# An adaLN block with a spectral filter: one slice of the modulation weights loaded in two parts, the second behind the fourth turning transfer

## The chip, the cores and the metric

The kernel runs on one core of a Trainium2 chip. The metric is the device time of one execution in microseconds; the time given for a kernel is the median of several runs. All times below are microseconds (us) from the start of the profiled span unless they are called device times.

## What is computed

A block with two branches, each with a layer norm, a modulation computed from a small vector `c`, and a gate, on x of 2048 tokens by 640 features in bf16:

```python
mod = (silu(c) @ w_mod).reshape(1, 6, 1, 640)
sa, ca, ga, sb, cb, gb = (mod[:, i] for i in range(6))
h = layernorm(x) * (1 + ca) + sa
y = irfft2(rfft2(h) * (w_r + 1j * w_i))          # over tokens and features
x = x + ga * y
h = layernorm(x) * (1 + cb) + sb
out = x + gb * ((silu(h @ w_gate) * (h @ w_up)) @ w_down)
```

`w_mod` has 640 rows and six slices of 640 columns. The order of the slices is sa, ca, ga, sb, cb, gb.

## The kernel before, in words

**Stages.** The two-dimensional Fourier transform is done by matrix products with cosine and sine tables. First comes the forward transform (loop at L482): tokens through `Mtab`, features through `Rs`, result `A_sb` in SBUF, 81 feature frequencies by 1024 values. Then `A_sb` has to be turned, so that the token frequencies lie in the free dimension. TensorE turns groups of four frequencies (`t2_pe`, L559), and four DMA transposes turn the rest (`t2_dma`, L539, issued at L549 to L552; called the four turning transfers here). Then a loop over 21 groups of up to four frequencies (L762) does the filter: `mix` (L577, matmuls at L583) into PSUM, `prod` (L599, VectorE at L607) times the filter weights, `stage_b` (L609, matmuls at L615, ScalarE copy at L618), `stage_c` (L633, matmuls at L645), `evac` (L647). GpSimd makes sums of weights (`wsum`, L421) and of products (`presum`, L621) in that time. A side line for the special frequencies runs in the same loop: `sp_gather` (L661, GpSimd at L663) reads all four turned pieces, then come `sp_mm` (L668) at groups 9, 11 and 13 and `sp_ev` (L691); its last step sends two small DMAs at L706 and L707. Then the inverse transform runs over 16 token tiles (L1258), each with a VectorE step at L1278 that adds the residual. After the third tile the second layer norm begins for the first two tiles, and at L1296 `ln2_tr(0)` issues a DMA transpose (line L878; called the h2 transpose here) whose result, modulated at L886 and L892, feeds the first products of the feed-forward part (`gu13`, L1090; `gu_plain`, L1102). The rest (L1132, L1003) is the feed-forward part in Strassen-like products, bound by TensorE.

**The modulation slices.** The vector `sc_col` is silu(c). `wm_ca` and `wm_sa` hold the slices of ca and sa. The other four lie in one tile `wm_r` of 5 x 4 x 640 (k block, slice, column) in the region rM: slice 0 is ga, 1 is sb, 2 is cb, 3 is gb. Slice 0 is used by `ga_mod` (L715, matmuls at L712). Slices 1 and 2 are used in pieces of 128 columns: in `mix`, behind the first matmul of a group, `mod_col` (L594, five matmuls at L596) makes one column piece `c5`, as this line orders it:

```python
for c5 in {8: (0,), 10: (1,), 12: (2,), 14: (3,), 16: (4,), 18: (5, 6), 20: (7, 8, 9)}.get(g, ()):
    mod_col(psum[:, 3 + 2 * (g % 2), 448 + c5:449 + c5], wm_r[:, :, 1 + c5 // NC5], c5 % NC5)
```

So group 8 reads columns 0 to 127 of slice 1, group 10 reads 128 to 255, group 12 reads 256 to 383, and so on; group 18 is the first to read slice 2. Slice 3 is read at the end of the loop (L814). `mix(g + 2)` is called in round g. TensorE takes its instructions in this written order.

**Queues.** Nearly all loads are issued by the SP queue, in the order of the program, and SP waits in order, too: an issue that waits for an engine holds back all issues behind it. The order around the change is: K tables, slice sa, slice 0, the special K table (L299), slice 1 (L300), then the four turning transfers (L549 to L552, all recorded at L543), the token table of the inverse transform (`Htab`, L553), its feature table (L554), slices 2 and 3 (L555, L556), the two small DMAs of the side line (L706, L707), the weights of the down product (L822 to L826), a small table (L829, L830), the gate and up weights (L834), the h2 transpose (L878). GpSimd issues some accumulating loads (L912).

Of the kernel before, what the change touches and what calls it, by code (L numbers as in the profile page):

```python
# [17 lines left out]
S, D, FF = 2048, 640, 1728  # L18
# [148 lines left out]
def adaln_block_kernel(ctx, tc, A_x, A_w_r, A_w_i, B_x, B_w_gate, B_w_up, B_w_down, c, w_mod, out):  # L167
    nc = tc.nc
# [57 lines left out]
    wm_r = rM.cut(12800, [NC5, 4, D])  # L226
# [68 lines left out]
    wm_m = wm_v[:, :, 2 * D:6 * D].rearrange("p k (i d) -> p k i d", i=4)  # L295
# [1 line left out]
    nc.sync.dma_start(wm_sa[:], wm_v[:, :, 0:D])  # L297
    nc.sync.dma_start(wm_r[:, :, 0, :], wm_m[:, :, 0, :])
    nc.sync.dma_start(Kstab[:], Ks_dram)  # L299
    nc.sync.dma_start(wm_r[:, :, 1, :], wm_m[:, :, 1, :])  # L300

    nc.vector.memset(ones[:], 1.0)
    nc.vector.memset(one11[:], 1.0)
# [29 lines left out]
    if True:  # L333
        def bn(ti, n=1, mid=None):
            for i in range(ti, ti + n):
                for k in range(2):
                    nc.vector.bn_stats(bn6a[:, i % 2, k, :], x_sb[:, i, 320 * k:320 * k + 320])  # L337
                    if i == ti + 1 and k == 0 and mid is not None:
                        if mid in (4,6,8):
                            xhat(mid, nc.vector)  # L340
                            xhat(mid + 1, nc.vector)
                        else:
                            xpair(mid)
            for i in range(ti, ti + n):
                nc.vector.bn_aggr(mv[:, i, :], bn6a[:, i % 2])
# [15 lines left out]
        def xpair(lo):  # L361
            nc.gpsimd.tensor_scalar(nmean[:, lo:lo + 2], mv[:, lo:lo + 2, 0], -1.0, 0.0, ALU.mult, ALU.add)
            xhat(lo, nc.gpsimd)
            xhat(lo + 1, nc.vector)

        def xhat(ti, eng):
            o, xi, r = xhs[ti // 2 % 3][:, ti % 2], x_sb[:, ti, :], rstd[:, ti:ti + 1]
            if eng is nc.vector:
                eng.tensor_scalar(o, xi, mv[:, ti, 0:1], r, ALU.subtract, ALU.mult)  # L369
            else:  # L370
                eng.tensor_scalar(o, xi, nmean[:, ti:ti + 1], r, ALU.add, ALU.mult)
# [80 lines left out]
        idle_pe(6, 2)  # L452
        nc.scalar.activation(sc_f[:], cps, ACT.Silu)
        bn(0, 2)
        rstd_of(0, 2)
        nc.vector.tensor_copy(sc_col[:], sc_f[:])
        mps = psum[:, 3, 32:32 + 32 * NC5]
        act_stats(3)
        for r in range(4):
            nc.scalar.mul(Rs[:, 1, r, :], Rp[:, 4, :], mask4[:, r:r + 1])  # L460
        bn(2)
        rstd_of(2, 1)
        xhat(0, nc.vector)
# [5 lines left out]
        xhat(2, nc.vector)  # L469
        xhat(3, nc.vector)  # L470
        bn(4, 2)
        idle_pe(4, 2)
        mod_cols(mps, wm_ca, range(0, 3), 32)
# [62 lines left out]
    if True:  # L536
        B2of = {}

        def t2_dma(bi):  # L539
            l0 = (1, 16, 32, 64)[bi]  # L540
            n = 15 if bi == 0 else 16
            B2b = rL.cut(4096 * bi, [16, 128]) if bi < 3 else rM.cut(6144, [16, 128])
            nc.sync.dma_start_transpose(B2b[:, :n, :], A_sb[:, l0:l0 + n].rearrange("p l t k c r -> p l (t k c r)"))  # L543
            for i in range(n):
                B2of[l0 + i] = (B2b, i)
            spec.append((B2b, n, slice(l0, l0 + n)))
# [3 lines left out]
        t2_dma(1)  # L550
        t2_dma(2)
        t2_dma(3)  # L552
        nc.sync.dma_start(Htab.rearrange("p (t h) v k -> p t h (v k)", h=2)[:, :, 0, :], H_dram.rearrange("p t v k -> p t (v k)"))  # L553
        nc.sync.dma_start(RI[:], RI_dram)  # L554
        nc.sync.dma_start(wm_r[:, :, 2, :], wm_m[:, :, 2, :])  # L555
# [808 lines left out]
@with_exitstack  # L1364
def kernel(
    ctx: ExitStack,
    tc: tile.TileContext,
    A_x: bass.AP,
    A_w_r: bass.AP,
    A_w_i: bass.AP,  # L1370
    B_x: bass.AP,
    B_w_gate: bass.AP,
    B_w_up: bass.AP,
    B_w_down: bass.AP,
    c: bass.AP,
    w_mod: bass.AP,
    out: bass.AP,
):
    with tc.manual_schedule():
        adaln_block_kernel(tc, A_x, A_w_r, A_w_i, B_x, B_w_gate, B_w_up, B_w_down, c, w_mod, out)  # L1380
# [30 lines left out]
```

## Time and profile before

| | us |
|---|---|
| median of 3 runs, device time | 247.27 (246.79 to 247.45) |
| the profiled execution, device time | 247.35 |
| its span in the profile | 245.6 |

The time outside the span is 247.35 - 245.6 = 1.75 us. Sums are made against the profiled execution. TensorE (PE) is busy for 96% of the span, VectorE (DVE) for 84%, ScalarE (ACT) for 69%, GpSimd (POOL) for 32%. "PEld" is TensorE's load of stationary weights, "SPq" the SP queue issuing.

### The profile page before, as it was taken

Reading aid. Unit: us, or ns where it says so; the run is one execution under the profiler, and the core shown is the slowest. Engines: PE = TensorE matmul, PEld = TensorE weight load, DVE = VectorE, ACT = ScalarE, POOL = GpSimd, SP = SyncE. Lnnn points to the kernel's source line nnn. Section 1 sums busy time; section 2 is a strip of 40 time slices with the busy share of each in tenths; the row PEclk is TensorE's granted clock in tenths of the full one; section 3 lists DMA queues with packets and bytes.
Section 4 is the critical chain, followed back from the end, with each engine's and each line's share of the span. In section 5 each row is a group of like instructions: output and inputs, shape, how many; then the busy total and the mean of one; then the engine's idle time right before and its main releaser. Section 6 shows DMA issues by size and latency. Waiting matters only on the chain.

```text
span 245.6 us, 5940 instructions
## 1 busy us (share of the span) xinstructions
PE 236.9 (96%) x2221; PEld 186.0 (76%) x2221; DVE 205.5 (84%) x485; ACT 170.2 (69%) x338; POOL 78.8 (32%) x122
## 2 busy tenths in 40 slices
PE   8899999899999999999999999999999999999994
PEld 2777889799997887788887778887765665666773
DVE  4898988797699995989989968788998777789864
ACT  3898877899997887588864588765247787773220
POOL 3637997698615414002004400001422000004400
PEclk9999999999999999999999999999999999999999
DMA  7999989989999899600005110202411000000111
GB/s 207 373 342 305 349 183 157 261 240 355 327 317 256 166 245 189 138 1 3 0 3 107 56 56 0 56 1 41 91 31 56 0 0 1 3 1 0 56 53 53
DMA packets 44142, 31.19 MB, mean 127 GB/s; under 512 B 21873, under 2 KB 41810, under 8 KB 44114
## 3 DMA queue, kind: packets, MB, share of 16 engines
q1 hardware_dynamic: 42176, 26.15, 41.2%
q0 software_dynamic: 1376, 4.26, 7.6%
q10 hardware_dynamic: 562, 0.41, 0.5%
q8 instruction: 17, 0.28, 0.5%
q14 instruction: 11, 0.09, 0.1%
HBM read 23.49 MB, written 2.62 MB: 106 GB/s over the span
## 4 chain that ended last, share of the span: by engine, by line
PE 79%; DVE 7%; POOL 5%; DMA 4%; issue 3%; ACT 0%; SPq 0%; DVEq 0%; POOLq 0%
PE psum L1132 36%; PE psum L1003 19%; PE psum L1102 6%; PE psum L980 3%; DMA rW<-rL 3%; DVE bn6a L337 3%; PE psum L615 2%; PE psum L583 2%; PE psum L1090 2%; PE psum L404 1%; DMA rX<-in_A_x_dram 1%; DVE rE L369 1%; PE psum L645 1%; POOL rL L1285 1%; DVE rM L607 1%
## 5 line engine op out<-in xcount | busy, mean ns | idle before, releaser
L1132 PEld LDWEIGHTS <-rW 128*128 128x128 bf16 (+1 forms) x429 | 42.0, 98 | 12.6
L1132 PE MATMUL psum<-rW 128*128 128x256 bf16 (+1 forms) x247 | 42.2, 287 | 0.0
L1029 POOL TENSOR_TENSOR rM<-rM,rL 128x320 f32<-128x320 f32 x6 | 5.4, 906 | 96.6 <-ACT rL L1028 96.6
L1003 PEld LDWEIGHTS <-rE 128*128 128x128 f16 (+1 forms) x196 | 19.0, 97 | 7.8
L1003 PE MATMUL psum<-rE 128*128 128x320 f16 (+1 forms) x147 | 22.9, 299 | 0.0
L607 DVE TENSOR_TENSOR rM<-psum,rW 128x384 bf16<-128x384 f32 (+2 forms) x42 | 20.4, 544 | 2.8 <-PE psum L583 2.8
L1170 ACT COPY rX<-psum 128x384 f32<-128x384 f32 (+2 forms) x27 | 14.0, 520 | 7.5 <-PE psum L1132 7.4
L1132 PEld LDWEIGHTS <-rE 128*128 128x128 f16 x156 | 15.3, 98 | 4.7
L1163 ACT COPY rH<-psum 128x384 f32<-128x384 f32 (+2 forms) x27 | 14.0, 517 | 7.0 <-PE psum L1132 6.3
L1167 DVE TENSOR_TENSOR rH<-psum,rM 128x512 bf16<-128x512 f32 (+1 forms) x24 | 15.0, 624 | 4.1 <-PE psum L1132 2.2
L1186 ACT ACTIVATE rL<-psum 128x384 bf16<-128x384 f32 (+2 forms) x27 | 14.4, 533 | 5.4 <-PE psum L1132 3.4
L1171 DVE TENSOR_TENSOR rX<-psum,rX 128x384 f32<-128x384 f32 (+2 forms) x27 | 16.3, 604 | 1.6 <-ACT rX L1170 1.4
L1157 ACT COPY rM<-psum 128x384 f32<-128x384 f32 (+2 forms) x27 | 13.9, 516 | 3.7 <-PE psum L1132 3.7
L1278 DVE SCALAR_TENSOR_TENSOR rM<-psum,rX 128x640 f32<-128x640 f32 x16 | 13.1, 821 | 3.8 <-PE psum L737 2.5
L1132 PE MATMUL psum<-rW,rE 128*128 128x256 bf16 (+1 forms) x78 | 15.6, 290 | 0.0
L1132 PE MATMUL psum<-rE,rY 128*128 128x256 f16 (+1 forms) x78 | 15.6, 290 | 0.0
L1187 ACT ACTIVATE rL<-rX 128x384 bf16<-128x384 f32 (+2 forms) x27 | 15.1, 558 | 0.0
L337 DVE BATCH_NORM_STATS2 bn6a<-rX 128x6 f32<-128x320 bf16 x30 | 13.1, 480 | 2.2 <-DMA rX<-in_A_x_dram 2.2
L1102 PE MATMUL psum<-rW 128*128 128x256 bf16 x130 | 14.4, 273 | 0.0
L972 DVE TENSOR_TENSOR rA<-psum,rM 128x320 bf16<-128x320 f32 (+1 forms) x27 | 12.1, 472 | 2.4 <-PE psum L980 2.3
L1102 PEld LDWEIGHTS <-rW 128*128 128x128 bf16 x130 | 12.7, 98 | 1.4
L424 POOL TENSOR_TENSOR rW<-rW 128x256 bf16<-128x256 bf16 x20 | 13.4, 700 | 0.7 <-DVE rW L393 0.5
(235 smaller groups left out, 640.0 us busy)
## 6 DMA issues: line engine op xcount, KB each, us to landing
rM<-in_w_mod_dram SPq DMA_DIRECT2D x4, 800.0 KB, 8.3
out_dram<-rA SPq DMA_DIRECT2D x31, 80.0 KB, 1.6
rX<-in_A_x_dram SPq DMA_DIRECT2D x6, 320.0 KB, 5.6
rA<-in_B_w_down_dram SPq DMA_DIRECT2D x2, 960.0 KB, 5.4
rY<-in_B_w_gate_dram POOLq DMA_DIRECT2D x2, 832.0 KB, 7.7
rW<-in_B_w_gate_dram SPq DMA_DIRECT2D x1, 1440.0 KB, 10.5
rW<-in_A_w_i_dram SPq DMA_DIRECT2D x2, 642.0 KB, 10.8
rW<-in_A_w_r_dram SPq DMA_DIRECT2D x2, 642.0 KB, 10.2
```

Source lines behind the costliest of these rows:

```text
L337: nc.vector.bn_stats(bn6a[:, i % 2, k, :], x_sb[:, i, 320 * k:320 * k + 320])
L607: nc.vector.tensor_tensor(PPs[g][:, v0:v1, hl], xv[:, v0:v1, hl], in1, ALU.mult)
L1003: nc.tensor.matmul(o, lhsT=lhs[rows(k), k], rhs=rhs[rows(k), k], start=start and k == ks[0], stop=stop and k == ks[-1], skip_group_check=True)
L1102: nc.tensor.matmul(gu[u], lhsT=Wgu[:, u, c5, ff * 128:(ff + 1) * 128], rhs=h2T[:, :, c5, :], start=(c5 == 0), stop=(c5 == NC5 - 1))
L1132: nc.tensor.matmul(o[:, f], lhsT=w, rhs=b, start=(start and f == 0 and i == 0), stop=(stop and f == len(groups[g]) - 1 and i == len(ops) - ...
L1157: nc.scalar.copy(c0, X)
L1163: nc.scalar.copy(c2, X)
L1167: nc.vector.tensor_tensor(c11, Z, c0, ALU.add)
L1170: nc.scalar.copy(c3, X)
L1171: nc.vector.tensor_tensor(c22, Y, c3, ALU.add)
L1186: nc.scalar.activation(g21, X, ACT.Silu, scale=-1.0)
L1187: nc.scalar.activation(g22, c22, ACT.Silu, scale=-1.0)
```

## The change

Slice 1 of `wm_r` is loaded in two parts: columns 0 to 255 in the old place, ahead of the turning transfers, and columns 256 to 639 right behind the fourth turning transfer, ahead of `Htab`. The other line of the diff only sets spaces in a tuple.

```diff
@@ -297,7 +297,7 @@
     nc.sync.dma_start(wm_r[:, :, 0, :], wm_m[:, :, 0, :])
     nc.sync.dma_start(Kstab[:], Ks_dram)
-    nc.sync.dma_start(wm_r[:, :, 1, :], wm_m[:, :, 1, :])
+    nc.sync.dma_start(wm_r[:, :, 1, 0:256], wm_m[:, :, 1, 0:256])
@@ -336,7 +336,7 @@
-                        if mid in (4,6,8):
+                        if mid in (4, 6, 8):
@@ -550,6 +550,7 @@
         t2_dma(2)
         t2_dma(3)
+        nc.sync.dma_start(wm_r[:, :, 1, 256:D], wm_m[:, :, 1, 256:D])
         nc.sync.dma_start(Htab.rearrange("p (t h) v k -> p t h (v k)", h=2)[:, :, 0, :], H_dram.rearrange("p t v k -> p t (v k)"))
         nc.sync.dma_start(RI[:], RI_dram)
         nc.sync.dma_start(wm_r[:, :, 2, :], wm_m[:, :, 2, :])
```

## The prediction

> **What bounds the kernel now.** I read the page's busy times first, then the chain of waits, then SP's issues with their landing times, then the DMA rate by stretches.
>
> ```profile
> PE 236.9 (96%) x2221; PEld 186.0 (76%) x2221; DVE 205.5 (84%) x485; ACT 170.2 (69%) x338; POOL 78.8 (32%) x122
> PE 79%; DVE 7%; POOL 5%; DMA 4%; issue 3%; ACT 0%; SPq 0%; DVEq 0%; POOLq 0%
> ```
>
> TensorE bounds the kernel. In the chain (second line) DMA holds 4%; most of that is one piece, seen in the chain in order of time (start, length, what):
>
> ```profile
> 69.49 7.04 DMA rW<-rL
> ...
> 80.20 14.19 PE psum L1102 x130
> ```
>
> From 80.20 on TensorE has work to the end, so what moves that start moves the end. Last to arrive ahead of it was the h2 transpose, issued at 69.49 and landed at 69.49 + 7.04 = 76.53. The timeline says how long TensorE waited for what follows from it:
>
> ```profile
> 79.27 0.38 PE L1090 MATMUL psum<-rW,Wp 128*128 128x256 bf16 x2 [0.61 <-POOL rW L886]
> ```
>
> So TensorE came 0.61 us before the modulated h2. Two paths meet here: TensorE's own, with 0.61 us to spare, and the h2 transpose, with nothing to spare. The change must be priced on both.
>
> Now the place of the change: SP's issues (start, length), with one line of SP's waits behind them.
>
> ```profile
> 24.80 0.71 SPq L300 DMA_DIRECT2D rM<-in_w_mod_dram  x1
> 32.44 7.70 SPq L543 DMA_TRANSPOSE rL<-rA  x3
> 40.31 3.08 SPq L543 DMA_TRANSPOSE rM<-rA  x1
> 43.44 0.65 SPq L553 DMA_DIRECT2D rH<-tab_H  x1
> ...
> 44.83 0.42 SPq L555 DMA_DIRECT2D rM<-in_w_mod_dram  x1
> 45.31 0.52 SPq L556 DMA_DIRECT2D rM<-in_w_mod_dram  x1
> 51.77 0.54 SPq L706 DMA_DIRECT2D rE<-rE  x1
> ...
> 53.07 1.12 SPq L822 DMA_DIRECT2D rA<-in_B_w_down_dram  x2
> ```
> ```profile
> SPq L543 <- DVE rA L419: 6.9, 1, 6.9
> ```
>
> The first turning transfer isn't held back in SP by slice 1: SP had issued slice 1 by 25.5 and then waited 6.9 us for VectorE to finish `A_sb`. Is it held back in the DMA engines? I compare it with a transpose on an idle queue much later (windows: length, PE, PEld, DVE, ACT, POOL busy, clock, DMA share, GB/s):
>
> ```profile
> 32.44:33.64 1.20, 1.20 (x27) 1.07 (x24) 0.54 (x4) 1.14 (x3) 0.67 (x2) 1.00 0.05 13
> 129.55:130.72 1.17, 1.17 (x11) 0.73 (x9) 1.10 (x4) 0.57 (x2) 0.03 (x1) 1.00 0.00 0
> ```
> ```profile
> 129.55 3.10 SPq L878 DMA_TRANSPOSE rW<-rL  x1
> ```
>
> The transpose issued at 129.55 moves nothing for 1.17 us either, with nothing ahead of it. The first turning transfer waits about 1.2 us, in which the rest of slice 1 drains (13 GB/s). So slice 1 is out of the way before the transfers could begin, and taking 60% of it away frees at most some 0.1 us. That is the main point against a gain.
>
> Do the turning transfers matter? Yes, the fourth:
>
> ```profile
> 45.20 0.97 POOL L663 TENSOR_TENSOR rE<-rM,SA 128x16 bf16<-128x16 bf16 x6 [1.24 <-DMA rM<-rA]
> ```
>
> GpSimd waits 1.24 us for it, and TensorE for GpSimd. Were the transfers late because of slice 1, up to about 1 us could be won. By the windows above they aren't.
>
> **The change part by part.** *Removed from the front:* 384 of 640 columns, 800 x 0.6 = 480 KB, ahead of the transfers. Its readers had it long before. I cost this at 0 (bounds: 0.1 us gained by the windows above; nothing lost).
>
> *First part, 320 KB, read by groups 8 and 10.* Does group 8 now wait for the second part as well, being the same tile? Slice 0 answers (start, length):
>
> ```profile
> 36.26 0.84 PE L712 MATMUL psum<-rM,sc_rep 128*128 128x320 bf16 x5
> ```
>
> These products read slice 0 at 36.26, though the loads of slices 2 and 3 into the same tile stand ahead of them in the program and were issued only at 44.83 and 45.31. Waits go by the columns. Cost 0.
>
> *Second part, 480 KB, issued at 43.44 where `Htab` was.* When does it land, and when is it wanted? Landing times of `Htab`, its follower and slice 2 (KB, us from issue), then TensorE's weight loads:
>
> ```profile
> rH<-tab_H SPq DMA_DIRECT2D x1, 512.0 KB, 4.8
> ```
> ```profile
> rH<-tab_RI SPq DMA_DIRECT2D x1, 320.0 KB, 5.0
> ```
> ```profile
> rM<-in_w_mod_dram SPq DMA_DIRECT2D x1, 800.0 KB, 8.1
> ```
> ```profile
> 47.39 0.25 PEld L596 LDWEIGHTS <-rM 128*128 128x128 bf16 x5
> ...
> 48.55 0.21 PEld L645 LDWEIGHTS <-rY 128*128 128x128 bf16 x3 [0.22 <-issue]
> ...
> 53.64 0.38 PEld L596 LDWEIGHTS <-rM 128*128 128x128 bf16 x10
> ...
> 54.31 0.26 PEld L615 LDWEIGHTS <-rE 128*128 128x128 bf16 x4 [0.16 <-POOL rE L624]
> ```
>
> The L596 rows are in order: group 8, 10, 12 and so on; the one at 47.39 is group 12, the first to read column 256. `Htab` in this slot landed at 43.44 + 4.8 = 48.24. The second part has 32 KB less, at 353 GB/s (a row below) 0.09 us: 48.15. TensorE then waits 48.15 - 47.39 = 0.76 us. Bounds: 0, if it lands within 3.95 us; and 1.05 us, with the 5.0 us of the row behind `Htab`. I take 0.76, since the slot and the size are `Htab`'s.
>
> Queued behind that matmul on TensorE are the rest of group 12's `mix`, `stage_b` and `stage_c`. `stage_c` had its own gap of 0.22 us at 48.55, which vanishes into the new wait: net 0.76 - 0.22 = 0.54.
>
> The Trainium skill ("DMA: Bandwidth & Descriptors", the section on the anatomy of one DMA) fits one DMA as about 2.0 us plus bytes over 436 GB/s. For the second part that would be an estimate of 3.1 us, so 46.6, and no wait at all; for `Htab` it would be 3.2 us, and this trace shows 4.8. The measurement decides, and the page's result is a rival below.
>
> *The queue behind it.* `Htab`, RI and slices 2 and 3 come later by what 480 KB take. Rates (last column, GB/s):
>
> ```profile
> 45.00:46.00 1.00, 0.36 (x7) 0.19 (x4) 0.43 (x1) 0.75 (x2) 0.80 (x6) 1.00 0.34 47
> 46.00:52.00 6.00, 5.68 (x99) 5.51 (x100) 5.03 (x16) 4.97 (x10) 5.23 (x9) 1.00 1.07 353
> 53.00:54.00 1.00, 1.00 (x25) 1.00 (x23) 1.00 (x4) 1.00 (x3) 1.00 (x2) 1.00 0.24 29
> 54.00:55.00 1.00, 1.00 (x20) 0.84 (x17) 1.00 (x4) 0.76 (x3) 1.00 (x2) 1.00 0.67 56
> 55.00:72.00 17.00, 16.94 (x280) 15.82 (x277) 12.68 (x31) 15.37 (x30) 10.02 (x13) 1.00 1.09 348
> 72.00:76.00 4.00, 4.00 (x62) 3.73 (x61) 3.70 (x9) 3.79 (x9) 0.00 (x0) 1.00 1.35 120
> ```
>
> 480 KB are 0.49 MB; at 353 GB/s, 1.39 us. The extra issue on SP (0.42 to 0.71 us by its neighbours' rows) hides in that. `Htab` then lands at 48.24 + 1.39 = 49.6; its first reader is GpSimd, much later:
>
> ```profile
> 54.24 1.11 POOL L785 TENSOR_SCALAR rH<-rH,sgnc 128x1024 bf16<-128x1024 bf16 x1
> ```
>
> So 0 for `Htab`; RI is read after it, slice 3 only behind the last group. Slice 2 is tight: it landed at 44.83 + 8.1 = 52.93 and comes at 54.32; group 18 wants it at 53.64 + 0.54 = 54.18. Another 0.14 us. TensorE then is 0.68 us late, and the gap of 0.16 at 54.31 can take back some: I take 0.6. Bounds: 0, if what makes the second part land in time brings slice 2 forward, too; and 1.05, the upper end of the first wait with no gap that takes any back (slice 2 is in time then).
>
> The Trainium skill (same page, Bandwidth) wants loads batched to 1 MiB or more and gives 341 GB/s at 1 MB and 138 at 64 KB. By it the split loses rate; at an estimated 240 GB/s the 480 KB would take 2.05 us. Here the loads of 320 to 800 KB in 46 to 52 run at 353, so the trace disagrees.
>
> *Does the delay reach the h2 transpose?* From 55 to 72 the DMA engines run full (DMA share 1.09), and the transpose's data come only after that (120 GB/s from 72 on): a queue that starts later drains later. But at 53 to 55 it moves only about 85 KB in 2 us; at 353 GB/s that leaves (706 - 85) / 353 = 1.76 us free. SP issued nothing between 45.31 and 51.77, and the down weights only at 53.07; with 1.2 us to first data, as in the windows above, they couldn't flow before 54.3. I read the pause as a queue run dry, and 1.39 fits into 1.76. What then moves the 55 us start is SP: the DMA at 51.77 waits for VectorE's step below, and VectorE, busy for 5.03 of the 6 us from 46 to 52, takes that step behind its products of group 12:
>
> ```profile
> 51.34 0.29 DVE L705 CAST rE<-psum 128x40 bf16<-128x40 f32 x2
> ```
>
> TensorE's 0.54 passes through VectorE to SP nearly whole, so the down weights and all behind them come about 0.5 us later, and the h2 transpose lands 0.5 us later (bounds 0 and 1.39). TensorE's own 0.6 fits into the 0.61 us it had to spare. L1090 therefore starts 0.5 later, and so does the end.
>
> **Sum:** 247.35 + 0.76 - 0.22 (the gap), with the 0.14 of slice 2 lost in TensorE's spare time, is 247.35 + 0.5 = 247.85. The profiled execution stands 0.08 above the median of 247.27; for a median I say 247.8.
>
> **The rivals.** *The queue passes it on (slower).* Place: the pause at 53 to 55. If more than 1.76 - 1.39 = 0.37 us of it are start-up that recurs however full the queue is, the rest adds up; if all of it recurs, the h2 transpose comes 1.39 late: 247.27 + 1.39 = 248.7. For it: the other slow second, 45 to 46 at 47 GB/s, had loads waiting (issued 43.44 to 45.31) and wasn't dry. Against: the 1.2 us to first data explain most of the pause.
>
> *No trace left.* The second part lands within 3.95 us, as the skill's fit has it; the slow second at 45 to 46 would have to be `Htab`'s own. Then neither path moves: 247.3.
>
> *The transfers come earlier (faster).* If slice 1's tail holds the first turning transfer by up to 0.9 us in spite of the idle-queue row, the 1.24 us wait shrinks by as much, and TensorE is 0.9 - 0.6 = 0.3 early. The end gains only if the h2 transpose, too, is earlier, and at most 0.61 + 0.3 = 0.9: about 246.4.
>
> *It doesn't act by columns.* Group 8, whose turn comes in the round of L663 (45.20), waits for the second part until 48.15: 3 us or more, 250 and up. The L712 row speaks against it.
>
> **How the numbers follow.** About 0.3% (0.74 us) can be told from no change. Forecast (247.4 to 248.3): 0.52, of which 0.15 lies above 248.0. Queue passes it on: 0.22. No trace left: 0.15. Faster: 0.09. Not by columns: 0.02. Faster 0.09; same 0.37 + 0.15 = 0.52; slower 0.15 + 0.22 + 0.02 = 0.39. The range takes in the first three, from 247.0 to 249.0 (0.3 beyond the second case).
>
> **What would show it.** Right: L596 of group 12 with a wait on the second part near 0.8 us; the fourth transfer's wait at L663 still 1.2; the pause at 53 to 55 filled; L1090 at about 79.8 still waiting for L886. Wrong: a first turning transfer that moves data before 33.5; no wait at L596; or a pause as long as before, with the h2 transpose landing near 77.9.

## The result, and the profile after

| | before | changed |
|---|---|---|
| median, first comparison (6 runs each) | 246.83 (246.24 to 247.45) | 248.99 (248.74 to 249.96) |
| ratio, first comparison | | 1.0077 [1.0049, 1.0106] |
| median, second comparison (23 and 10 runs, below) | 246.78 (246.17 to 248.06) | 248.08 (246.90 to 250.26) |
| ratio, second comparison | | 1.0059 [1.0033, 1.0086] |
| profiled execution, device time | 247.35 | 249.0 |
| its span | 245.6 | 247.2 |

The change costs 1.3 to 2.2 us. The forecast was 247.8 and the range 247.0 to 249.0: the direction was right, the size too small. The first median stands 0.01 us below the upper end of the range, so that it lies inside is luck; the second, 248.08, lies well inside.

I read the profile after in the order of the prediction. First the page's busy times and the shares of the chain that ended last:

```profile
PE 237.8 (96%) x2221; PEld 186.2 (75%) x2221; DVE 205.7 (83%) x485; ACT 170.0 (69%) x338; POOL 78.7 (32%) x122
...
PE 80%; DMA 9%; DVE 4%; POOL 3%; issue 1%; ACT 1%; SPq 0%; ACTq 0%; DVEq 0%; POOLq 0%
```

No engine has more work to speak of, but DMA's share of the chain went from 4% to 9%. The changed kernel's chain around the change, in order of time (start, length, what), says what is new in it:

```profile
43.33 5.31 DMA rM<-in_w_mod_dram
...
48.68 0.28 PE psum L597 x5
```

The second part of slice 1 now lies on the chain: issued at 43.33, landed 5.31 us later at 48.64, and TensorE's group 12 (L596 is L597 after) goes on with it. The timeline of TensorE's weight loads gives the wait in brackets:

```profile
48.67 0.19 PEld L597 LDWEIGHTS <-rM 128*128 128x128 bf16 x5 [1.40 <-DMA rM<-in_w_mod_dram]
...
50.61 0.26 PEld L597 LDWEIGHTS <-rM 128*128 128x128 bf16 x5
...
54.60 0.38 PEld L597 LDWEIGHTS <-rM 128*128 128x128 bf16 x10
```

It is 1.40 us, where 0.76 was forecast. The next piece, group 14 at 50.61, comes 0.96 later than in before:

```profile
49.65 0.26 PEld L596 LDWEIGHTS <-rM 128*128 128x128 bf16 x5
```

Groups 8 and 10 show no such wait (waits go by the columns), and group 18, at 54.60, none on slice 2. How it goes on is seen in SP's issues, a line later in the code than before:

```profile
40.23 3.06 SPq L543 DMA_TRANSPOSE rM<-rA  x1
...
52.73 0.54 SPq L707 DMA_DIRECT2D rE<-rE  x1
54.12 1.12 SPq L823 DMA_DIRECT2D rA<-in_B_w_down_dram  x2
70.43 1.99 SPq L879 DMA_TRANSPOSE rW<-rL  x1
```

The fourth turning transfer (40.23) is issued as in before (40.31). The two small DMAs come at 52.73 instead of 51.77 (0.96 later), the down weights 1.05 later, the h2 transpose 0.94 later. The chain at the end of that stretch, and TensorE's timeline there:

```profile
69.87 0.53 DVE rL L865
...
70.43 7.92 DMA rW<-rL
...
78.54 2.40 POOL rW L887 x4
...
80.98 0.38 PE psum L1091 x2
```
```profile
79.68 0.27 PE L1091 MATMUL psum<-rW,Wp 128*128 128x256 bf16 x1 [0.27 <-POOL rW L887]
80.44 0.27 PE L1091 MATMUL psum<-rW,Wp 128*128 128x256 bf16 x1 [0.49 <-POOL rW L887]
80.98 0.38 PE L1091 MATMUL psum<-rW,Wp 128*128 128x256 bf16 x2 [0.27 <-POOL rW L887]
```

The chain comes to the h2 transpose from VectorE's step of the second layer norm (L865), not from an issue of SP: it is issued late because TensorE, and behind it the layer norm, are late. The transpose took 7.92 us instead of 7.04. So it lands 0.94 + 0.88 = 1.82 later, at 78.35 instead of 76.53, the matmuls behind it come 80.98 - 79.27 = 1.71 later, and the device time is 249.0 - 247.35 = 1.65 longer. TensorE, although late itself, still waits 0.27 + 0.49 + 0.27 = 1.03 us there: it isn't its own lateness that sets the end.

The DMA rate by stretches in the changed kernel (last column GB/s), for the pause and for the first turning transfer:

```profile
32.34:33.54 1.20, 1.20 (x27) 1.08 (x24) 0.55 (x3) 1.14 (x3) 0.67 (x2) 1.00 0.02 7
54.00:55.00 1.00, 1.00 (x24) 1.00 (x23) 1.00 (x4) 1.00 (x2) 1.00 (x2) 1.00 0.39 70
55.00:56.00 1.00, 1.00 (x20) 0.84 (x17) 1.00 (x3) 0.83 (x3) 1.00 (x2) 1.00 0.57 77
```

With 480 KB less ahead of it, the first turning transfer still moves nothing for its first 1.2 us (7 GB/s, before 13). GpSimd's wait for the fourth transfer is the same, too (1.24 before; timeline of GpSimd):

```profile
45.11 0.98 POOL L664 TENSOR_TENSOR rE<-rM,SA 128x16 bf16<-128x16 bf16 x6 [1.26 <-DMA rM<-rA]
```

The pause is still there: before it was 53 to 55 at 29 and 56 GB/s, now 54 to 56 at 70 and 77. That alone doesn't say that the 480 KB found no room in it, for SP issues the down weights 1.05 us later, which by itself would lengthen the pause. The bytes are counted under e2 below.

### The profile page after: what moved, and what is told of

Same layout as the page of the kernel before. It is cut to its first block, busy times and chain, and to the rows that moved or that the text cites. A ratio compares the mean times of both kernels' runs of the same rounds, so it can differ in the third digit from the quotient of the medians.

```text
span 247.2 us, 5943 instructions
## 1 busy us (share of the span) xinstructions
PE 237.8 (96%) x2221; PEld 186.2 (75%) x2221; DVE 205.7 (83%) x485; ACT 170.0 (69%) x338; POOL 78.7 (32%) x122
## 4 chain that ended last, share of the span: by engine, by line
PE 80%; DMA 9%; DVE 4%; POOL 3%; issue 1%; ACT 1%; SPq 0%; ACTq 0%; DVEq 0%; POOLq 0%
PE psum L1133 36%; PE psum L1004 19%; PE psum L1103 6%; DMA rX<-in_A_x_dram 4%; DMA rW<-rL 3%; PE psum L981 3%; PE psum L616 3%; PE psum L584 2%; DMA rM<-in_w_mod_dram 2%; DVE bn6a L337 2%; PE psum L1091 2%; PE psum L646 1%; PE psum L404 1%; POOL rL L1286 1%; POOL rW L887 1%
## 5 line engine op out<-in xcount | busy, mean ns | idle before, releaser
L619 ACT CAST rY<-psum 128x512 bf16<-128x512 f32 (+2 forms) x21 | 11.9, 576 | 3.5 <-PE psum L616 3.3
```

## The experiments

My theory after the result: two costs, both of which reach the end by the h2 transpose. *The wait*: group 12 holds TensorE, hence VectorE and SP, and the down weights are issued late. *The bytes*: 480 KB more stand in the queue ahead of the h2 transpose, and it takes longer from issue to landing. The rivals: the wait alone (the prediction's forecast), the bytes alone ("the queue passes it on"), and a cost of splitting as such.

| run | median, us (runs) | before beside it | ratio |
|---|---|---|---|
| e1_split_ahead | 247.11 (12) | 246.84 | 1.0013 [1.0002, 1.0025] |
| e2_read_later | 247.71 (6) | 246.84 | 1.0041 [1.0025, 1.0058] |
| e3_behind_htab | 249.42 (6) | 246.84 | 1.0108 [1.0074, 1.0142] |
| e4_up_behind_h2 | 246.88 (12) | 246.84 | 0.9998 [0.9985, 1.0011] |
| e5_htab_first | 247.59 (12) | 246.85 | 1.0029 [1.0018, 1.0040] |
| e6_split384 | 247.20 (12) | 246.85 | 1.0008 [0.9996, 1.0021] |
| e7_before_up_behind_h2 | 246.38 (12) | 246.85 | 0.9988 [0.9973, 1.0002] |
| e8_later_up_behind_h2 | 246.19 (12) | 246.85 | 0.9973 [0.9960, 0.9985] |
| e9_change_again | 248.08 (10) | 246.78 | 1.0059 [1.0033, 1.0086] |
| e10_wait_up_behind_h2 | 247.47 (7) | 246.78 | 1.0020 [1.0000, 1.0040] |
| e11_small_table_behind_h2 | 246.51 (12) | 246.78 | 0.9993 [0.9982, 1.0003] |

**Splitting alone.** Both parts stay ahead of the turning transfers.

```diff
     nc.sync.dma_start(wm_r[:, :, 1, 0:256], wm_m[:, :, 1, 0:256])
+    nc.sync.dma_start(wm_r[:, :, 1, 256:D], wm_m[:, :, 1, 256:D])
...
-        nc.sync.dma_start(wm_r[:, :, 1, 256:D], wm_m[:, :, 1, 256:D])
```

> Slice 1 in two parts, both ahead of the turning transfers. Theory 'the wait' (TensorE waits at group 12 for the second part, and the loop, SP and the h2 transpose follow it): no wait, so the time of before, 246.8 +-0.4. Theory 'the queue' (0.49 MB behind the fourth transfer push all later loads, whatever TensorE does): also 246.8 +-0.4, since nothing is moved behind the transfers. If the split itself costs (rows of 512 and 768 bytes, one DMA more): 247.5 or more.

Measured 247.11, 0.27 us above before by the medians (at most 0.6 by the interval) for one more DMA. The rest of the cost lies in the place of the second part.

**The bytes without the wait.** The change, but the column piece 2 is made in group 14 instead of group 12, when the second part has long landed.

```diff
-                    for c5 in {8: (0,), 10: (1,), 12: (2,), 14: (3,), 16: (4,), 18: (5, 6), 20: (7, 8, 9)}.get(g, ()):
+                    for c5 in {8: (0,), 10: (1,), 14: (2, 3), 16: (4,), 18: (5, 6), 20: (7, 8, 9)}.get(g, ()):
```

> The changed kernel, with the column piece 2 made in group 14 beside piece 3, not in group 12; the loads stay as changed. 'The wait': TensorE wants column 256 about 2.2 us later, by when it has landed; the loop is on time, so the small DMAs at L707 come at about 51.8 and the time is 247.0 +-0.4. 'The queue': the 0.49 MB are still ahead of everything, the h2 transpose lands 1.4 us or more later than before, 248.3 to 249.

Measured 247.71, 0.87 above before, with no wait at the modulation products. That is between the two numbers expected and fits neither. SP's down weights and the chain's transpose in this kernel:

```profile
53.49 1.12 SPq L823 DMA_DIRECT2D rA<-in_B_w_down_dram  x2
```
```profile
69.97 7.64 DMA rW<-rL
```

I measure how much longer the h2 transpose is held by the time from the down weights' issue to its landing, which leaves out how late SP was. Before: 76.53 - 53.07 = 23.46. Here: 69.97 + 7.64 - 53.49 = 24.12, which is 0.66 us more. "The wait alone" falls. The split alone (e1), with nothing pushed back, has 68.72 + 7.06 - 52.21 = 23.57:

```profile
52.21 1.12 SPq L823 DMA_DIRECT2D rA<-in_B_w_down_dram  x2
```
```profile
68.72 7.06 DMA rW<-rL
```

Do the 0.66 us arise because the pause doesn't take the bytes up? The windows answer, laid by the down weights' issue: from 45.00 to 1.5 us behind that issue, the next 6 us, and the next 5.5 us; in before, in this kernel and in the changed kernel.

```profile
45.00:54.57 9.57, 8.61 (x150) 8.03 (x148) 8.03 (x23) 8.27 (x14) 8.60 (x16) 1.00 0.88 264
54.57:60.57 6.00, 6.00 (x127) 5.87 (x125) 5.04 (x11) 5.22 (x10) 5.73 (x5) 1.00 0.98 340
60.57:66.07 5.50, 5.44 (x83) 5.00 (x81) 2.69 (x7) 5.09 (x12) 2.30 (x5) 1.00 1.15 294
```
```profile
45.00:54.99 9.99, 8.89 (x153) 8.44 (x153) 8.43 (x24) 8.57 (x14) 8.70 (x16) 1.00 1.02 302
54.99:60.99 6.00, 6.00 (x126) 5.87 (x124) 5.07 (x11) 5.36 (x10) 5.62 (x5) 1.00 1.01 339
60.99:66.49 5.50, 5.27 (x81) 4.88 (x77) 2.63 (x7) 4.92 (x11) 2.22 (x5) 1.00 1.18 281
```
```profile
45.00:55.62 10.62, 8.62 (x149) 7.91 (x147) 8.11 (x23) 8.18 (x14) 8.69 (x16) 1.00 0.92 282
55.62:61.62 6.00, 6.00 (x127) 5.87 (x125) 4.95 (x11) 5.28 (x9) 5.66 (x5) 1.00 0.99 341
61.62:67.12 5.50, 5.48 (x84) 5.00 (x82) 2.77 (x8) 5.11 (x12) 2.40 (x5) 1.00 1.13 246
```

The first rows moved 9.57 x 264 = 2526, 9.99 x 302 = 3017 and 10.62 x 282 = 2995 thousand bytes: 491 and 469 more than before, and 480 KB are 492. So nearly all pushed bytes have moved within 1.5 us of the down weights' issue, as in the prediction, and the 6 us behind that run at 340, 339 and 341 GB/s, alike. The queue falls behind only in the third stretch, at 294, 281 and 246. For the changed kernel that is 5.5 x (294 - 246) / 340 = 0.78 us, all that it is late by this measure (78.35 - 54.12 = 24.23, against 23.46: 0.77). For e2 it is 0.21 of the 0.66; the rest isn't placed. The same stretch in two kernels further down that push nothing back, e7 and, with the small table (L829, L830) behind the h2 transpose as well, e11:

```profile
60.15:65.65 5.50, 5.48 (x83) 5.00 (x81) 2.69 (x7) 5.12 (x12) 2.31 (x5) 1.00 1.16 252
```
```profile
59.91:65.41 5.50, 5.48 (x83) 5.00 (x81) 2.69 (x7) 5.11 (x12) 2.31 (x5) 1.00 1.09 336
```

e11 differs from e7 in the place of the small table alone, so the stretch is slow when that table's loads are in it. But e7, with no bytes pushed back, is nearly as slow there as the changed kernel. That the second part costs time without any wait of TensorE is shown by e2's median; by what way 480 KB that have long moved would slow that stretch is not.

**The wait without the bytes.** `Htab` (512 KB) takes the place of the second part ahead of the transfers, so that behind them stands nearly as much as before (32 KB less).

```diff
+    nc.sync.dma_start(Htab.rearrange("p (t h) v k -> p t h (v k)", h=2)[:, :, 0, :], H_dram.rearrange("p t v k -> p t (v k)"))
     nc.sync.dma_start(wm_r[:, :, 1, 0:256], wm_m[:, :, 1, 0:256])
...
         nc.sync.dma_start(wm_r[:, :, 1, 256:D], wm_m[:, :, 1, 256:D])
-        nc.sync.dma_start(Htab.rearrange("p (t h) v k -> p t h (v k)", h=2)[:, :, 0, :], H_dram.rearrange("p t v k -> p t (v k)"))
```

> The changed kernel, with the token table (512 KB) issued ahead of the turning transfers, in front of the first part of slice 1: ahead of the transfers stand 32 KB more than before the change, behind them 32 KB less, so the wait of TensorE is left alone without bytes pushed back. Theory 'both halves' (the wait costs about 1.1 us, the bytes in the queue about 0.9): TensorE waits 0.8 to 1.4 us at group 12 and the time is 1.1 above before, 247.9 +-0.4. 'The wait' alone as cause: 249.0. 'The queue' alone: 246.8.

Measured 247.59, 0.74 above before. Its weight load of group 12, its down weights and its h2 transpose:

```profile
48.08 0.19 PEld L597 LDWEIGHTS <-rM 128*128 128x128 bf16 x5 [0.73 <-DMA rM<-in_w_mod_dram]
```
```profile
53.49 1.12 SPq L823 DMA_DIRECT2D rA<-in_B_w_down_dram  x2
```
```profile
70.12 6.90 DMA rW<-rL
```

The wait is there, 0.73 us, and 70.12 + 6.90 - 53.49 = 23.53: the h2 transpose is held no longer than in before (23.46) and e1 (23.57). "The bytes alone" falls, too. The two costs together, 0.87 + 0.74 = 1.61 us, lie between the 1.30 and the 2.16 of the two comparisons of the change.

**Fewer bytes, no wait.** The cut at column 384: 320 KB go behind the transfers, and group 12 finds its columns in the first part.

```diff
-    nc.sync.dma_start(wm_r[:, :, 1, 0:256], wm_m[:, :, 1, 0:256])
+    nc.sync.dma_start(wm_r[:, :, 1, 0:384], wm_m[:, :, 1, 0:384])
...
-        nc.sync.dma_start(wm_r[:, :, 1, 256:D], wm_m[:, :, 1, 256:D])
+        nc.sync.dma_start(wm_r[:, :, 1, 384:D], wm_m[:, :, 1, 384:D])
```

> The changed kernel, cut at column 384, not 256: 480 KB ahead, 320 KB behind the fourth transfer, first read by group 14, 2.2 us later than group 12. No wait of TensorE, 0.33 MB pushed back. 'Both halves': two thirds of the queue's 0.9 us, 247.4 +-0.4. 'The wait' alone: 246.9. 'The queue' alone (2.1 us for 0.49 MB): 248.2.

Measured 247.20, 0.35 above before by the medians; the interval takes in no change, so the time alone doesn't part the 247.4 of both halves from the 246.9 of the wait. Its rows:

```profile
52.39 1.12 SPq L823 DMA_DIRECT2D rA<-in_B_w_down_dram  x2
```
```profile
68.80 7.69 DMA rW<-rL
```

68.80 + 7.69 - 52.39 = 24.10: the h2 transpose is held as long as with 480 KB. The size of the bytes' cost doesn't follow their number in single profiles; that they cost something is shown by e2 against before, how much per KB isn't.

**A longer wait.** The second part behind `Htab`.

```diff
-        nc.sync.dma_start(wm_r[:, :, 1, 256:D], wm_m[:, :, 1, 256:D])
         nc.sync.dma_start(Htab.rearrange("p (t h) v k -> p t h (v k)", h=2)[:, :, 0, :], H_dram.rearrange("p t v k -> p t (v k)"))
+        nc.sync.dma_start(wm_r[:, :, 1, 256:D], wm_m[:, :, 1, 256:D])
```

> The changed kernel, with the second part issued behind the token table, not ahead of it: the same bytes in the same stretch of the queue, but the second part lands some 1.4 us later (about 50). 'The wait': TensorE waits 2.7 us instead of 1.3 and the time is 1.2 to 1.5 us above the changed kernel, about 250.3. 'The queue': as the changed kernel, 249.0 +-0.4.

Measured 249.42: three runs from 248.0 to 248.61 and three from 250.24 to 250.72. The median is less than I had expected, and so was the wait in the profile, which is of a run at 248.46. Weight load, down weights, transpose, and the slow stretch:

```profile
48.71 0.19 PEld L597 LDWEIGHTS <-rM 128*128 128x128 bf16 x5 [1.99 <-DMA rM<-in_w_mod_dram]
```
```profile
54.13 1.11 SPq L823 DMA_DIRECT2D rA<-in_B_w_down_dram  x2
```
```profile
70.64 7.09 DMA rW<-rL
```
```profile
61.63:67.13 5.50, 5.28 (x80) 4.89 (x78) 2.60 (x7) 4.93 (x11) 2.20 (x5) 1.00 1.15 295
```

In this execution the bytes cost nothing: 70.64 + 7.09 - 54.13 = 23.60, and the slow stretch runs at 295 GB/s, as in before (294). The down weights were issued as late as in the changed kernel (54.13 and 54.12), which lost 0.77 us there, so SP's lateness alone doesn't make the difference; what does stays open.

**Where both costs reach the end.** The change, with 640 KB of up weights taken from ahead of the h2 transpose and issued right behind it.

```diff
     load_gu(512, 1664, (0,))
-    load_gu(0, 512, (1,))
...
                 ln2_tr(0)
+                load_gu(0, 512, (1,))
                 load_gu(512, 1024, (1,))
```

> The changed kernel, with the first 640 KB of the up weights issued behind the h2 transpose, not ahead of it. If the h2 transpose sets the end because of what is queued ahead of it: it starts some 1.8 us earlier, TensorE (0.95 us late, with 0.61 to spare) sets the start of the feed-forward part, and the time is 247.2 +-0.4. If TensorE's own lateness is what sets the end: no gain, 249.

Measured 246.88: the time of before, though the second part still comes behind the transfers and TensorE still waits. TensorE's waits in it:

```profile
47.44 0.19 PEld L597 LDWEIGHTS <-rM 128*128 128x128 bf16 x5 [0.34 <-DMA rM<-in_w_mod_dram]
...
53.72 0.32 PEld L597 LDWEIGHTS <-rM 128*128 128x128 bf16 x10 [0.31 <-DMA rM<-in_w_mod_dram]
```

The second row is group 18 on slice 2: the wait that the prediction put at 0.14 does occur. To tell what this edit gives by itself, it was made in before, and in e2 (bytes, no wait) and in e5 (wait, no bytes):

> The kernel before, with the first 640 KB of the up weights issued behind the h2 transpose. If the h2 transpose sets the start of the feed-forward part and TensorE has 0.61 us to spare there: 246.2 +-0.3, faster than before. If something else ends last there: 246.8.

> The changed kernel with column piece 2 made in group 14 (no wait) and the 640 KB of up weights behind the h2 transpose (less ahead of it). If what the bytes cost is only the h2 transpose's start: both causes are gone, 246.3 +-0.4, as the kernel before with the same reordering. If the bytes cost TensorE something elsewhere (slice 2 late, say): 247 or more.

> The wait alone (token table ahead of the transfers, second part in its slot), with the 640 KB of up weights behind the h2 transpose, so that TensorE and not the h2 transpose sets the start of the feed-forward part. 'Both halves': TensorE's wait passes to the end nearly whole, 0.5 to 0.9 us above the kernel before with the same reordering (246.4): 247.1 +-0.3. If the wait costs only by way of SP's later loads and the h2 transpose: 246.4.

e7: 246.38, an interval that just takes in no change. e8: 246.19, faster than both kernels. The first products behind the h2 transpose in e7, then in e8, have no bracket, that is no wait:

```profile
77.67 0.71 PE L1089 MATMUL psum<-rW,Wp 128*128 128x256 bf16 x5
```
```profile
77.77 0.71 PE L1090 MATMUL psum<-rW,Wp 128*128 128x256 bf16 x5
```

In e8 the h2 transpose lands 5.5 us after its issue, where e2 has 7.64 (KB left out for a transpose, us):

```profile
rW<-rL SPq DMA_TRANSPOSE x1, 5.5
```

So with less ahead of the h2 transpose no cost of the bytes is seen (e8 against e7, 246.19 and 246.38). The wait does cost: e10 took 247.47, 1.09 above e7 by the medians and about 0.8 by the ratios to the before beside each (the two weren't measured side by side). Its weight load shows

```profile
48.32 0.19 PEld L597 LDWEIGHTS <-rM 128*128 128x128 bf16 x5 [1.19 <-DMA rM<-in_w_mod_dram]
```

Then it is TensorE itself that is late. The theory needs that correction: the bytes act by the h2 transpose, as far as these runs show, the wait by either path. That e4, with both, took 0.6 less than e10 goes with the waits of their profiles (0.34 + 0.31 against 1.19); that this spread is the whole reason isn't shown.

**More of the same?** Before, with the up weights and the small table (L829, L830) behind the h2 transpose.

> The kernel before, with the 640 KB of up weights and the two loads of the small table (128-byte rows) behind the h2 transpose. If TensorE alone sets the start once the up weights are out of the way: no further gain, 246.3 +-0.3. If the queue still holds the h2 transpose back: 245.9. If the small table now comes too late for L1090: 247 or more.

Measured 246.51: no further gain beside e7's 246.38.

**The change once more,** for its spread.

> The changed kernel once more (only the spaces in the tuple are set back), for the size of the effect and for how much TensorE's wait and the h2 transpose's landing vary between executions: 248.8 +-0.4; a wait at group 12 between 0.7 and 1.4 us; the h2 transpose lands 1 to 2 us later than before. If the first measurement was high by chance: 248.0 or less.

Measured 248.08, from 246.90 to 250.26: below the 248.8 +-0.4 that I expected, and 0.9 below the first comparison. Its profile is of the execution at 246.90. The issues of the fourth turning transfer and of the second part, how the latter landed (KB, us), group 12, and two rows further down:

```profile
38.51 3.77 SPq L543 DMA_TRANSPOSE rM<-rA  x1
42.32 0.58 SPq L553 DMA_DIRECT2D rM<-in_w_mod_dram  x1
```
```profile
rM<-in_w_mod_dram SPq DMA_DIRECT2D x1, 480.0 KB, 4.4
```
```profile
46.82 0.26 PEld L597 LDWEIGHTS <-rM 128*128 128x128 bf16 x5
```

```profile
52.32 1.12 SPq L823 DMA_DIRECT2D rA<-in_B_w_down_dram  x2
```
```profile
68.72 7.53 DMA rW<-rL
```

The last two are its down weights and its h2 transpose, which lands at 76.25, not 1 to 2 us later than before (76.53) as expected. TensorE doesn't wait at all, where I had expected 0.7 to 1.4: 42.32 + 4.4 = 46.72, and group 12 starts at 46.82. The same program waits 1.40 us in one execution and not in another, depending on when the fourth transfer let SP go (42.32 or 43.33) and how long the second part took (4.4 or 5.3 us).

## Why the prediction was right, and where it was too small

- *Removed from the front: 0.* Right. The first turning transfer moves nothing in its first 1.2 us in either kernel, and GpSimd's wait for the fourth is 1.24 and 1.26. "The transfers come earlier" is refuted.
- *First part by columns: 0.* Right: groups 8 and 10 don't wait.
- *The wait, 0.76 (0 to 1.05).* Right in kind, mis-sized, and its upper bound too low: 1.40 in the profiled execution, 0.34 and 0 in others of the same place. I took one landing time (4.8) and one issue time (43.44) as constants. The landing measured 4.3 (e5), 4.4 (e9) and 5.3; the estimate by the Trainium skill's fit ("DMA: Bandwidth & Descriptors", the anatomy of one DMA) was 3.1, and no trace here comes near it. That section of the Trainium skill gives the fit for DMAs that GpSimd issues; this load is issued by SP, which the prediction passed over. A single execution (e9) came without the wait, as in "no trace left", but the landing took 4.4 us, not under 3.95: SP had issued the load early, at 42.32.
- *Slice 2 late by 0.14.* Small either way: 0 in the profile after, where TensorE comes later to group 18 (54.60 instead of 53.64), 0.31 in e4.
- *The split itself, 0.* The prediction read from the rate of 353 GB/s that it costs nothing; e1 measured 0.27 us (at most 0.6), with both parts ahead of the transfers.
- *The flight of the h2 transpose, 7.04 unchanged.* This is the step that failed: with the pause taken as room for the 1.39 us, the sum put nothing on the way from the down weights to the h2 landing. That way is 23.46 to 23.60 us in before, e1, e5 and e3, and 23.93 to 24.23 in the others that push bytes back and keep the old order of the up weights (e9: 68.72 + 7.53 - 52.32 = 23.93; after: 78.35 - 54.12 = 24.23; e2 and e6 between), 0.33 to 0.77 us more.
- *1.39 fits into 1.76.* Right by the count of bytes under e2: what is pushed back has moved when the down weights begin. The prediction named as a sign against itself a pause as long as before, with the h2 transpose landing near 77.9. Both came (78.35), but the pause stayed long because SP was late, and the time is lost in the stretch that the small table slows, 246 instead of 294 GB/s, for which the prediction had no term. The rival "the queue passes it on" had the direction and, with 248.7, came nearer to the first median; the place that it named, the pause, isn't where the time was lost.
- *SP's lateness reaches the h2 transpose.* Right in size: 0.96 at SP's first late issue, 0.94 at the transpose. The path was only half of it. The issue of the transpose follows VectorE's layer norm on the chain, so group 12's delay reaches it through the computation, too, and not only through SP's down weights. Both come equally late, and no run here parts them.
- *TensorE's own lateness fits into its spare time.* Right: it still waits 1.03 us for the modulated h2.

With the two terms as the profiled execution has them, 0.94 at the issue of the transpose (from a wait of 1.40, of which 0.96 are left at group 14) and 0.88 in its flight, the sum is 247.35 + 1.82 = 249.2, against 249.0. Why the stretch with the small table runs at 246 GB/s in one execution and at 295 in another stays open: what stood in each DMA ring isn't seen in the trace, and nothing was tried on it.

## What to carry to other kernels

A load that is out of the way before its successor can start gains nothing by being moved, as slice 1 here; look at what the successor moves in its first microsecond. Moved behind transfers, it takes over their spread and pushes whatever stands last in that queue, so price it at the transfer that ends last (here the h2 transpose, issued 27 us later). To find where a queue lost time, lay the windows of two kernels by the same issue and count the bytes; a pause that looks as long as before may still have taken the bytes up, if the next issue came later. And look at what stands ahead of that last transfer without need: with one load of 640 KB moved behind it, piece 2 read two groups later and slice 1 split as in the change, the time was 246.19, 0.9973 [0.9960, 0.9985] of before.

## What the runs showed of the hardware

The fourth turning transfer of the same program was issued at 38.51 in one execution (e9) and at 40.23 in another (the profile after), and the load behind it at 42.32 and 43.33: 1.0 us apart, not much less than the change costs. A single profile of this kernel can't size a wait that hangs on it: the time from 246.90 to 250.26 of one program is wider than any difference in the table above. The queue's stretch with the small table's loads (rows of 128 bytes) ran at 246 (the changed kernel) to 295 GB/s (e3) with the table in it, and at 336 with the table moved out of it (e11).
